# A sliding-window attention and SwiGLU kernel: V's places in SBUF given by the order of their last reading, and x of units 17 to 19 transposed by DMA

## The chip, the core and the metric

The kernel runs on one NeuronCore of one Trainium2 chip, as one launch. The metric is device time in microseconds (us), median of several runs. The engines are named as in the profile: PE is TensorE (PEld its weight loads), DVE is VectorE, ACT is ScalarE, POOL is GpSimd, SP is SyncE. SP and POOL do no arithmetic here: they issue DMAs.

## The reference

Attention with a causal window of 128 and ALiBi slopes over 8 batches, 8 heads, 576 tokens, head size 64, and then a gated MLP over the 4608 tokens:

```python
scores = scale * np.matmul(q, k.transpose(0, 1, 3, 2))
mask = (rel >= 0) & (rel < window)            # rel = query position - key position, window = 128
scores = np.where(mask, scores + bias[None], -1e9)
attn = softmax(scores); attn_out = np.matmul(attn, v)
x = attn_out.transpose(0, 2, 1, 3).reshape(B * S, H * D)     # 4608 x 512
g = x @ w_gate                                # 512 x 1536
val = x @ w_val
out = (silu(g) * val) @ w_out                 # 1536 x 512, float32
```

## The kernel before

The attention is cut into 36 **units** of 128 tokens, `units[i] = (s, p)` with i = 9 s + p: s is a pair of batches, p = 0 to 3 the four whole tiles of the first batch, 4 to 7 those of the second, and p = 8 the two last half tiles of 64 tokens together. A **rank** is the same numbering for loaded tiles of q, k and v (all eight heads, 128 x 512).

A load (`load_qk`, L184, and `load_v`, L179) is a DMA issued by POOL, float32 in HBM to fp16 in SBUF. Tiles of q and k go to the pool `nat`, five places for each. Tiles of v go to twelve fixed places `va_all`, in turn: `va[rank] = va_all[rank % NV]` (L180). POOL issues its DMAs in a fixed order, for each rank k, q, v; it is an in-order queue, so a load whose place isn't free yet holds all loads behind it. No more than eight of POOL's DMAs are in flight, since each waits for the landing of the eighth before it.

From rank 11 on (`QK_DMA_FROM`), q and k are transposed by a DMA that SP issues (L236), into `kT` (12 places) and `qT` (9 places). SP too is an in-order queue; it also issues the stores of the output (L459).

`scores(i)` multiplies kT and qT into four PSUM tiles of the pool `ps_a` (4 places), ACT takes the exponent, VectorE applies the mask. `weighted(i)` (L337) multiplies with `va` into two PSUM tiles `av`, also of `ps_a`; VectorE divides by the sums (L360, L361) and writes the unit's `x`. `x` has three places (`xpool`, tag "x"), so unit i writes where the x of unit i - 3 lay. V of a rank is read by its own unit and the next one; of the ranks with c = 3 (c = rank % 9) it is also read by the unit p = 8 of the same pair, and the same holds for c = 7, which comes right before.

`x_transposed(i)` (L371) brings x into `xT`, the input of the MLP, in blocks of four units (block 8 holds the four units p = 8). For units below `X_DMA_FROM` = 22, PE transposes it in four matmuls into a PSUM tile `px` of `ps_a` (L385) and ACT copies it out (L389). In the generator `attention` this comes one unit late, by the list `waiting` (L894). From unit 22 on SP issues one DMA that transposes x directly (L379).

The MLP goes over nine blocks of 512 tokens: gate and val products (L413, `pg` and `pv`, PSUM pool `ps_f`, three places), tanh on ACT (L431), `uu` and `hT` on VectorE (L432, L443), and the product with w_out by a scheme with seven products for eight (L548), whose sums VectorE makes (L501 to L504). Blocks 6 to 8 do the gate and val products that way as well (L637).

PE's order is written out by hand: `everything` (L983) interleaves the steps of the MLP with those of the attention. POOL's order is fixed too. ACT, VectorE and SP are ordered by a scheduler, which plans with its own estimates of when things are ready; on the chip each engine then follows that order strictly.

Of the kernel before, what the change touches and what calls it, by code (L numbers as in the profile page):

```python
# [16 lines left out]
P = 128  # L17
WIN = 128
QK_DMA_FROM = 11
X_DMA_FROM = 22  # L20
MASKS_AT = (3.0, 5.0, 6.0, 7.0)
ALONE = 8
MANUAL = "compute"
# [27 lines left out]
def kernel(  # L51
# [98 lines left out]
    NV = 12  # L150
    VROW = 80
    va_all = []
# [12 lines left out]
    natq, natk, va = {}, {}, {}  # L165
# [4 lines left out]
    def source(src, rank):  # L170

        s, c = divmod(rank, 9)
        if c == 8:
            return [((64 * n, 64 * n + 64),
                     src[2 * s + n, :, 512:576, :].rearrange("h p d -> p h d")) for n in range(2)]
        b, t = 2 * s + c // 4, c % 4
        return [((0, P), src[b, :, t * P:(t + 1) * P, :].rearrange("h p d -> p h d"))]

    def load_v(rank):  # L179
        va[rank] = va_all[rank % NV]  # L180
        for (p0, p1), src in source(v, rank):
            nc.gpsimd.dma_start(va[rank][p0:p1, :, 0:D], src)  # L182

# [7 lines left out]
    def load(rank):  # L191
        load_qk(rank)
        load_v(rank)
# [143 lines left out]
    def weighted(i):  # L337

        s, p = units[i]
        x = xpool.tile([P, H, D], FP16, name="x", tag="x")  # L340
        xs[i] = x
        for half in range(2):
            pool, tag = (ps_f, "gv") if i < FIRST else (ps_a, "a")
            av = pool.tile([P, 4, D + 1], FP32, name="av", tag=tag)
            todo = []
            for j in range(4):
                h = 4 * half + j
                if p == 8:
                    for n, kt in enumerate((3, 7, 8)):
                        todo.append((j, ex[(s, "c", n)][:, slot(h), :], va[9 * s + kt][:, h, 0:D + 1]))  # L350
                else:
                    if p not in (0, 4):
                        todo.append((j, ex[(s, p - 1)][:, slot(h), 128:256],
                                     va[9 * s + p - 1][:, h, 0:D + 1]))
                    todo.append((j, ex[(s, p)][:, slot(h), 0:128], va[9 * s + p][:, h, 0:D + 1]))
            for n, (j, w, val) in enumerate(todo):
                nc.tensor.matmul(av[:, j, :], w, val, start=(n == 0), stop=(n == len(todo) - 1))  # L357
            rec = xpool.tile([P, 4, 1], FP32, name="rec", tag="rec", bufs=4)
            with tc.high_priority() if i in (6, 7) else ExitStack():
                nc.vector.reciprocal(rec, av[:, :, D:D + 1])  # L360
                nc.vector.tensor_mul(x[:, 4 * half:4 * half + 4, :], av[:, :, 0:D],  # L361
                                     rec.broadcast_to([P, 4, D]))
# [3 lines left out]
    def place(i):  # L366

        s, p = units[i]
        return (8, s) if p == 8 else (2 * s + p // 4, p % 4)

    def x_transposed(i):  # L371
        n, j = place(i)
        if n not in xT:
            xT[n] = bpool.tile([P, NKB, 512], FP16, name="xT", tag="xTc" if n == 8 else "xT",
                               bufs=1 if n == 8 else 3)
        x = xs.pop(i).rearrange("p h d -> p (h d)")
        dst = xT[n][:, :, j * P:(j + 1) * P]
        if i >= X_DMA_FROM:
            nc.sync.dma_start_transpose(dst, x)  # L379
            return  # L380
        pool, tag, n = ((ps_f, "gv", 3) if i == 2 else (ps_f, "po", 1) if i < FIRST
                        else (ps_a, "a", 4))
        pt = pool.tile([P, NKB, P], FP16, name="px", tag=tag, bufs=n)
        for kb in range(NKB):
            nc.tensor.transpose(pt[:, kb, :], x[:, kb * P:(kb + 1) * P], idm if i < FIRST else idm2)  # L385
        if i < FIRST:
            nc.vector.tensor_copy(dst, pt)
        else:
            nc.scalar.copy(dst, pt)  # L389
# [418 lines left out]
    def loads_to(r):  # L808
        nonlocal loaded
        while loaded <= min(r, NR - 1):  # L810
            load(loaded)
            loaded += 1

    def transposes_to(n):
        nonlocal done_t
        while done_t < n:
            transpose(done_t)
            done_t += 1

    def ahead(i):  # L820

        n = need[min(i + 4, last)]
        while done_t < n and order[done_t][1] < loaded and order[done_t][1] >= QK_DMA_FROM:
            transposes_to(done_t + 1)

    def run(steps):
        for fs in steps:
            for f in fs:
                f()
            yield  # L830
# [7 lines left out]
    def first_tiles():  # L838
# [14 lines left out]
        for i in range(FIRST):  # L853
            if i + 1 < FIRST:
                for n, _ in enumerate(run(scores(i + 1))):
                    if n == 0 and i == 0:
                        begin_scores(2, 0, 0)
                        begin_scores(2, 0, 1)
                    if n == 0 and i + 2 < FIRST:
                        transposes_to(need[i + 2])  # L860
            else:
                later_masks()
                for m in range(2):
                    wide(0, m, "g", P)
            weighted(i)
            if 0 < i < FIRST - 1:
                x_transposed(i - 1)
        x_transposed(2)
        begin(4, 2)
        x_transposed(3)  # L870
        begin(4, 3)

    def attention():

        waiting = []
        transposes_to(need[FIRST])
        for _ in run(scores(FIRST)):
            yield FIRST
        for i in range(FIRST, last + 1):
            late = i >= LATE  # L880
            if i < last:
                transposes_to(need[i + 1])
                for n, _ in enumerate(run(scores(i + 1))):
                    yield i - len(waiting)
                    if n == 2 and late:
                        weighted(i)
                        yield i - len(waiting)
            if not late or i == last:
                weighted(i)
                yield i  # L890
            loads_to(i + 7)
            ahead(i)
            yield i - len(waiting)
            if late and i < X_DMA_FROM:  # L894
                if waiting:
                    x_transposed(waiting.pop(0))
                waiting.append(i)
                yield i
                yield i
                continue  # L900
            while waiting:
                x_transposed(waiting.pop(0))
            x_transposed(i)
            yield i
            yield i + 1
# [11 lines left out]
    load_qk(1, "qk")  # L917
    load_qk(2, "q")
    load_v(0)
    load_qk(2, "k")  # L920
    load_qk(3, "q")
    load_v(1)
    load_qk(3, "k")
    load_v(2)
# [32 lines left out]


    att = attention()
    done = n_att = 0  # L960
    ready = [4, 8, 13, 17, 22, 26, 31, 35, 36]
# [88 lines left out]
```

The softmax here doesn't subtract the row's maximum and nothing guards it: scores larger than these inputs give would overflow.

## Time and profile before

| | us |
|---|---|
| median of 3 runs | 336.18 (335.59 to 336.44) |
| profiled execution, its own time | 335.64 |
| span of the profiled execution | 333.9 |
| PE busy | 325.9 |
| VectorE busy | 274.2 |
| ACT busy | 206.9 |
| POOL busy | 111.0 |

The profiled execution's own time is 1.7 us above its span, which runs from the first instruction to the last. Times in the views are counted from the start of the span. A DMA's duration on SP's row is that of its issue; "landing" is when all its data has arrived. A wait is listed as engine, line, releaser, then total, times and longest.

### The profile page before, as it was taken

The page shows a single profiled execution, that of the slowest core. Times are in us where ns is not written, and L with a number is a line of the kernel's source. Part 1 is how long each engine was busy: PE and PEld are TensorE (multiplying, and loading weights), DVE is VectorE, ACT ScalarE, POOL GpSimd, SP SyncE. Part 2 cuts the span into 40 slices and gives each one's busy share as a digit, 9 for nine tenths or more (in the row PEclk, how much of TensorE's full clock was granted, in tenths as well). Part 3 has the DMA queues.
Part 4 walks back from the last instruction along what each step waited for, and adds up shares of the span by engine and source line. Part 5 has one row for each costly group of instructions (what it writes and reads, how often), then busy time and mean ns, then how long its engine had stood idle before and what let it go on. Part 6 is the DMA issues. An engine that isn't in the chain of part 4 may idle for free.

```text
span 333.9 us, 7719 instructions
## 1 busy us (share of the span) xinstructions
PE 325.9 (98%) x2955; PEld 218.5 (65%) x2955; DVE 274.2 (82%) x643; ACT 206.9 (62%) x413; POOL 111.0 (33%) x138
## 2 busy tenths in 40 slices
PE   8999999999999999999999999999999999999994
PEld 4665465544465655656655655666788888888883
DVE  4678878999797879988999999999855985775683
ACT  4976777464766657567456465563567667776650
POOL 8977776458964098551035000000000000000000
PEclk9999999999999999999999999999999999999999
DMA  9999999999999999999969532030100101011014
GB/s 154 175 179 175 177 185 164 122 142 184 141 170 159 140 195 162 160 168 155 179 128 152 117 34 81 16 96 17 65 29 36 64 2 65 25 41 65 0 65 127
DMA packets 161669, 37.64 MB, mean 113 GB/s; under 512 B 149472, under 2 KB 157280, under 8 KB 161632
## 3 DMA queue, kind: packets, MB, share of 16 engines
q0 software_dynamic: 118880, 18.62, 78.8%
q1 hardware_dynamic: 42064, 17.90, 27.8%
q10 hardware_dynamic: 688, 0.62, 0.6%
q8 instruction: 23, 0.38, 0.5%
q14 instruction: 14, 0.11, 0.1%
HBM read 37.91 MB, written 9.44 MB: 142 GB/s over the span
## 4 chain that ended last, share of the span: by engine, by line
PE 87%; DVE 8%; ACT 2%; issue 1%; DVEq 0%
PE po L548 19%; PE pg L413 17%; PE pv L413 16%; PE gX L637 9%; PE av L357 5%; PE gY L637 5%; PE ps L289 3%; PE p L548 3%; PE gZ L637 2%; DVE uu L432 2%; PE psc L325 2%; DVE hT L443 2%; PE po L467 2%; PE px L385 2%; DVE ex L301 1%
## 5 line engine op out<-in xcount | busy, mean ns | idle before, releaser
L413 PE MATMUL pv<-xT,wv_sb 128*128 128x512 f16 (+2 forms) x312 | 76.6, 363 | 0.3 <-DVE uu L432 0.2
L413 PE MATMUL pg<-xT,wg_sb 128*128 128x512 f16 (+2 forms) x324 | 76.5, 355 | 0.1
L431 ACT ACTIVATE tt<-pg 128x512 f16<-128x512 f32 x68 | 40.9, 603 | 44.6 <-PE pg L413 44.6
L295 ACT ACTIVATE ex<-ps 128x512 f16<-128x512 f32 x96 | 50.0, 608 | 7.4 <-PE ps L289 7.4
L432 DVE SCALAR_TENSOR_TENSOR uu<-tt,pg 128x512 f16<-128x512 f16 x67 | 45.6, 681 | 8.6 <-ACT tt L431 8.3
L443 DVE TENSOR_TENSOR hT<-uu,pv 128x512 f16<-128x512 f16 x68 | 46.2, 681 | 1.6
L182 POOL DMA_DIRECT2D va<-in_v_dram x40 | 34.5, 871 | 38.2 <-DMA out_dram<-osb 20.4
L548 PEld LDWEIGHTS <-hT 128*128 128x128 f16 x384 | 37.2, 98 | 10.7 <-issue 0.8
L413 PEld LDWEIGHTS <-wg_sb 128*128 128x128 f16 x324 | 28.5, 98 | 23.5 <-issue 2.2
L413 PEld LDWEIGHTS <-wv_sb 128*128 128x128 f16 x312 | 27.8, 98 | 24.4 <-issue 2.3
L188 POOL DMA_DIRECT2D kn<-in_k_dram x39 | 33.5, 863 | 18.8 <-DMA qT<-qn 6.2
L188 POOL DMA_DIRECT2D qn<-in_q_dram x39 | 33.6, 871 | 9.7 <-DMA va<-in_v_dram 4.7
L548 PEld LDWEIGHTS <-S 128*128 128x128 f16 x288 | 27.5, 98 | 7.5 <-issue 1.4
L301 DVE TENSOR_TENSOR ex<-ex,m_reg 128x1024 f16<-128x1024 f16 x42 | 28.5, 685 | 3.0 <-ACT ex L295 3.0
L361 DVE TENSOR_TENSOR x<-av,rec 128x256 f16<-128x256 f32 x72 | 28.5, 420 | 0.5
L548 PE MATMUL po<-T,S 128*128 128x256 f16 x192 | 25.9, 273 | 0.3 <-ACT u2s L574 0.3
L548 PE MATMUL po<-T,hT 128*128 128x256 f16 x192 | 26.0, 272 | 0.0
L329 ACT ACTIVATE exc<-psc 128x512 f16<-128x512 f32 x40 | 21.4, 608 | 3.2 <-PE psc L325 3.1
L691 DVE TENSOR_TENSOR hT<-s,v 128x512 f16<-128x512 f16 x18 | 7.6, 424 | 17.7 <-ACT s L690 17.7
L357 PEld LDWEIGHTS <-ex 128*128 128x128 f16 x384 | 17.5, 98 | 4.4 <-issue 1.0
L357 PE MATMUL av<-va,ex 128*128 128x65 f16 x384 | 19.3, 193 | 0.3 <-ACT ex L295 0.3
L289 PE MATMUL ps<-qT,kT 64*128 64x256 f16 x192 | 16.0, 272 | 0.9 <-DVE qT L220 0.6
(129 smaller groups left out, 534.1 us busy)
## 6 DMA issues: line engine op xcount, KB each, us to landing
out_dram<-osb SPq DMA_DIRECT2D x32, 256.0 KB, 2.4
va<-in_v_dram POOLq DMA_DIRECT2D x32, 128.0 KB, 6.9
qn<-in_q_dram POOLq DMA_DIRECT2D x31, 128.0 KB, 7.9
kn<-in_k_dram POOLq DMA_DIRECT2D x31, 128.0 KB, 7.3
wg_sb<-in_moe_w_gate_dram POOLq DMA_DIRECT2D x6, 256.0 KB, 7.6
wo_sb<-in_moe_w_out_dram POOLq DMA_DIRECT2D x3, 512.0 KB, 8.2
wv_sb<-in_moe_w_val_dram POOLq DMA_DIRECT2D x5, 256.0 KB, 7.6
kn<-in_k_dram POOLq DMA_DIRECT2D x8, 64.0 KB, 6.4
```

Source lines behind the costliest of these rows:

```text
L182: nc.gpsimd.dma_start(va[rank][p0:p1, :, 0:D], src)
L188: nc.gpsimd.dma_start(t_[p0:p1], src)
L295: nc.scalar.activation(e[:, o:o + 2, :], banks[q4][par], AF.Exp, scale=scale)
L301: nc.vector.tensor_mul(e[:, o, :], e[:, o, :], reg[:, o, :])
L357: nc.tensor.matmul(av[:, j, :], w, val, start=(n == 0), stop=(n == len(todo) - 1))
L361: nc.vector.tensor_mul(x[:, 4 * half:4 * half + 4, :], av[:, :, 0:D], rec.broadcast_to([P, 4, D]))
L413: nc.tensor.matmul(ps[:, c0:c1], w[:, kb, ms], xT[n][:, kb, c0:c1], start=(kb == 0 and c0 == 0), stop=(kb == NKB - 1 and c1 == 512), skip_ ...
L431: nc.scalar.activation(tt, pg[:, c0:c1], AF.Tanh, scale=0.5)
L432: nc.vector.scalar_tensor_tensor(out=uu, in0=tt, scalar=one if (n, m) == PIN else 1.0, in1=pg[:, c0:c1], op0=ALU.add, op1=ALU.mult)
L443: nc.vector.tensor_mul(hT[n][:, m, c0:c1], acted[(n, m)][1][:, c0:c1], pv[:, c0:c1])
L548: nc.tensor.matmul(dst, a[:, m, cols], b[:, m, :], start=(start and m == 0), stop=(m == HM - 1), skip_group_check=True)
L637: nc.tensor.matmul(dst[:, i, :], w[:, kb, c0 + i * P:c0 + (i + 1) * P], a[:, kb, :], start=(start and i == 0 and kb == 0), stop=(i == 1 an ...
```

## The change

`load_v` no longer takes V's places in turn. It keeps for each of the twelve places the unit that reads it last, and gives a new tile the place whose last reading comes first. And `X_DMA_FROM` becomes a set that holds the units 17, 18 and 19 besides 22 to 35, so that these three go by DMA from SP, without `waiting`; units 20 and 21 stay with PE.

```diff
-X_DMA_FROM = 22
+X_BY_DMA = {17, 18, 19} | set(range(22, 36))
...
+    free_at = [-1] * NV
+
     def load_v(rank):
-        va[rank] = va_all[rank % NV]
+
+        n = free_at.index(min(free_at))
+        free_at[n] = rank - rank % 9 + 8 if rank % 9 == 3 else rank + (rank % 9 < 8)
+        va[rank] = va_all[n]
...
-        if i >= X_DMA_FROM:
+        if i in X_BY_DMA:
             nc.sync.dma_start_transpose(dst, x)
             return
...
-            if late and i < X_DMA_FROM:
+            if late and i not in X_BY_DMA:
```

The unit whose reading of V must be over before a rank's V can be loaded, for the ranks where it changes most:

```
rank     15  16  17  18  24  25  26  27  28  30  33  34  35
before    8   5   6   7  17  14  15  16  17  19  26  23  24
after     5   6   7   8  14  15  16  17  17  19  23  24  25
```

What stands in SP's queue, as built (k27 is the transpose of K of rank 27, q27 that of Q, x17 that of unit 17's x, S a store; the start and the end, equal or nearly so, are left out):

```
before  k17 q17 S k18 q18 k19 q19 k20 q20 S k21 q21 k22 q22 k23 S q23 q24 k24 S S k25 q25 k26 q26 S
        k27 q27 k28 S q28 k29 q29 k30 q30 k31 k32 q31 q32 S S x22 q33 x23 k33 x24 S S x25 x26 k34 q34 k35 q35 x27
after   k17 q17 k18 q18 S k19 q19 k20 k21 S q20 S q21 k22 q22 k23 S q23 q24 k24 q25 k25 S k26 q26 S
        k27 q27 x17 k28 q28 k29 k30 x18 S q29 S x19 k31 q30 k32 q31 q32 S S x22 q33 x23 k33 q34 k34 x24 k35 S q35 S x25 x26 x27
```

On PE three groups of four transposing matmuls are gone, on ACT the three copies; the rest of PE's and ACT's order is the same, and VectorE's but for two pairs of neighbours that change places. POOL issues the same DMAs in the same order.

## The prediction

> **What bounds the kernel now.** I read the page's shares first, then the chain that ended last, then the busy times by stage, then the queues of POOL and SP.
>
> ```profile
> PE 325.9 (98%) x2955; PEld 218.5 (65%) x2955; DVE 274.2 (82%) x643; ACT 206.9 (62%) x413; POOL 111.0 (33%) x138
> DMA  9999999999999999999969532030100101011014
> PE 87%; DVE 8%; ACT 2%; issue 1%; DVEq 0%
> ```
>
> TensorE is busy 98% of the span, and the chain lies on it for 87%. The busy times by stage give PE 59.75 of the 60 us from 100 to 160 us: a microsecond for which PE waits is a microsecond of the end, and one that PE saves is saved. The second line says that the DMA engines are full for the first half of the span (20 slices of 8.35 us).
>
> POOL, which issues all loads, waits long twice for a place of V (engine, line, releaser; total, times, longest):
>
> ```profile
> POOL va L182 <- DMA out_dram<-osb: 20.4, 1, 20.4
> POOL va L182 <- PE av L357: 11.7, 2, 9.6
> ```
>
> The 9.6 us end at 116.58 (V of rank 24; its place is rank 12's, which unit 17 reads last, until 115.86), the 20.4 us at 172.27 (rank 33 in rank 21's place, last read by unit 26 until 171.54; the releaser named is not the true one). Nobody on PE waits for either: V of 24 is read at 146.57 and V of 33 at 212.76, 30 and 40 us later. And the DMA engines hardly noticed. In the DMA view of 114 to 120 us, 40 slices of 0.15 us, this is their busy share:
>
> ```profile
> DMA  9111119999999999999999997999999999999999
> ```
>
> Five slices, 0.75 us, are empty. The loads in flight and SP's transposes filled the rest.
>
> SP's queue and VectorE around the change (start, duration; SP's duration is the issue alone):
>
> ```profile
> 132.32 1.24 SPq L236 DMA_TRANSPOSE kT<-kn  x1
> 133.67 1.28 SPq L236 DMA_TRANSPOSE qT<-qn  x1
> ...
> 147.87 1.19 SPq L236 DMA_TRANSPOSE kT<-kn  x1
> 149.17 1.22 SPq L236 DMA_TRANSPOSE qT<-qn  x1
> ```
> ```profile
> 136.92 0.76 DVE L361 TENSOR_TENSOR x<-av,rec 128x256 f16<-128x256 f32 x2
> 137.59 0.41 DVE L504 TENSOR_TENSOR S<-hT,S 128x512 f16<-128x512 f16 x1
> 137.92 0.68 DVE L432 SCALAR_TENSOR_TENSOR uu<-tt,pg 128x512 f16<-128x512 f16 x1
> ...
> 141.32 0.76 DVE L361 TENSOR_TENSOR x<-av,rec 128x256 f16<-128x256 f32 x2
> ```
>
> Counted along the queue, the first two are K and Q of rank 27, the next two K and Q of rank 30. The two writes of x are units 20 and 21. Landing, in the answer for line 236 from 127 to 152 us, and for line 379 over the span:
>
> ```profile
> DMA to landing us min/median/max: 6.3/7.0/8.9
> ```
> ```profile
> DMA to landing us min/median/max: 2.4/2.4/5.6
> ```
>
> A transpose by DMA takes 7.0 us while loads run, and 2.4 us after them. The new ones fall into the first stretch.
>
> **What the Trainium skill says.** "DMA: Bandwidth & Descriptors", section "Issuing engines are not separate DMA queues": DMAs of SP and POOL run on the same 16 engines and interleave. The trace agrees: 7.0 against 2.4 us. "Perfetto Trace Analysis", "DMA Instruction — HWDGE": the profiled window of such an instruction is its issue, not the moving of data. It agrees: 1.19 us against 6.8 us for the transpose at 147.87. "TensorE: Matmul & The Clock Gate", Part 1: after an idle window of about 3.4 us the array runs at half clock until it has been busy as long. At the start of this trace seven matmuls of 512 columns took 3.17 us, 453 ns each, where four in mid-kernel take 0.86 us, 215 ns each.
>
> **The change, part by part.**
>
> *PE and ACT.* Twelve transposing matmuls go. One group of four costs 0.22 us on the chain:
>
> ```profile
> 131.09 0.22 PE px L385 x4
> 131.32 0.86 PE pg L413 x4
> ```
>
> Three groups: 0.67 us off PE. Three copies of 0.585 us leave ACT, 5.6 to 6.9 us busy of ten there: worth nothing to the end. The orders of PE, ACT and VectorE are otherwise the same but for two neighbour swaps on VectorE, worth nothing.
>
> *V's places.* Rank 24 now waits for unit 14 instead of 17, rank 33 for 23 instead of 26; rank 27 waits for 17 instead of 16, 34 and 35 for one unit more. For PE directly: nothing, covered by the 30 and 40 us. For what stands behind in POOL's queue (K and Q of 25 and on): these are paced by the DMA engines. The 0.75 us of empty slices and the two microseconds after, in which the share of the DMA falls to 1.3 from its usual 1.9, make about 1.4 us; K of rank 30 comes earlier by that, less about 0.6 us for x17 (131 KB at some 200 GB/s) ahead of it. Bounds: 0 and 3 us earlier (3.0 is the pause in landings, from Q of 24 at 117.9 to V of 24 at 120.9). I take 0.9: K of rank 30 is issued at 147.0.
>
> *The three transposes on SP.* Each takes 1.3 us of SP and waits for its x. What matters is where they stand: x17 behind K and Q of rank 27, x18 behind K of rank 30, x19 five places later (store, Q of 29, store between). SP issues in order, and those before wait for loads. x17: 132.32 - 0.9 + 1.3 + 1.3 = 134.0 us, though its x is ready at 118.04. x18: 147.0 + 1.3 = 148.3 us, ready at 124.97. Landing 7.2 and 6.4 us later (within 6.3 to 8.9): 141.2 and 154.7 us.
>
> *Who waits for that.* x has three places, so unit 20 writes where x17 lay, 21 where x18, 22 where x19; before, PE had read them by 125.2, 131.3 and 136.4. Now VectorE waits for the landing, and all its queue with it. Unit 20's write, 136.92 before, goes to 141.2. Queued behind it is uu (137.92 before), which frees the PSUM place of the pv at 140.07: PE stands there some 3 us. Unit 21's write, 141.32 before, goes to 154.7. That write also frees unit 21's two av places in PSUM, and the second of the score matmuls of unit 23 takes the first of these. They were here:
>
> ```profile
> 143.64 0.61 PE L289 MATMUL ps<-qT,kT 64*128 64x256 f16 x8
> ```
>
> The second starts near 143.70; now it can at 154.7 + 0.42 (one write) + 0.05 = 155.2. PE is 11.5 us late, and this includes the first stall and the 0.67 us, which only lengthen the wait. The pg after it (144.84) needs hT, queued behind x21 (1.37 us from its start to hT's end): 156.1 against PE's own 156.3, no more. Unit 22's write would stand at 159.6; x19 is issued 3.9 us after x18, at 152.2, and lands by 159.1: just hidden.
>
> *Clock.* PE stands about 3 us and then 8: after the second the skill's page has it at half clock for some 3.4 us, 1.7 us of work. No run here shows it in mid-kernel; bounds 0 and 3.2 (both stalls). I take 1.5.
>
> Sum: 335.64 + 11.5 + 1.5 = 348.6 us for the profiled execution, and the median of the runs lies 0.54 above that execution: **349.1 us**.
>
> **Rivals.**
> 1. *No stall* (the other side): SP gets to the new transposes early, because POOL no longer stands 9.6 us. For it: that wait is right there. Against it: the DMA engines were full meanwhile. It decides at x18 landing by 143.70 - 0.67 - 0.47 = 142.6, that is K of rank 30 issued by 134.9, 13 us earlier than now; 9.6 us isn't enough. Then only the 0.67 us remain, and perhaps 0.24 us of score matmuls that waited for places at 137.2: 335.3 us in the median.
> 2. *Loads gain it all*: K of rank 30 comes 9.6 us earlier, at 138.3; x18 lands at 146.6, PE is 3.4 us late, without a clock loss: 339.6. Against it, the same DMA row.
> 3. *The lag goes on*: x19 lands late too, and VectorE, busy 29.9 of 30 us from 160 to 190, can't make up its lag; another 3 to 6 us: 352 to 355.
> That the change doesn't do what it says is excluded by the built order: twelve matmuls fewer, three more transposes on SP, VectorE's three writes waiting for them.
>
> **How the numbers follow.** The stall as worked out 0.76, rival 3 0.06, rival 2 0.11, rival 1 0.07. A measurement of this kernel can tell about 0.3%, 1.0 us: rival 1 lies just inside, so faster 0.03, same 0.04, slower 0.93. For the likeliest case: early end, K of 30 comes 3 us earlier, a landing of 6.3 us, no clock loss: x18 at 152.5, 9.2 us late, 345.4; late end, no gain, 0.6 us more for x17, a landing of 8.9 us and 3.2 us of clock: 158.7, 15.4 + 3.2, 354.8. The range 343 to 354 holds nearly all of that and part of rivals 2 and 3.
>
> **What would show it.** Right: VectorE idle before x at units 20 and 21, some 4 and 9 us, released by the DMA of xT; PE idle at pv or uu near 140 and at ps near 144, near 11 us in all; a dip in PEclk after it; POOL's two long waits for va gone; x18 issued right behind a kT at about 147. Wrong: kT of rank 30 issued before 140, no idle on VectorE, or a PE that runs through it.

## The result, and the profile after

| | before | after |
|---|---|---|
| median, us | 335.71 (335.28 to 336.44, 6 runs) | 349.16 (348.66 to 349.99, 6 runs) |
| profiled execution, its own time | 335.64 | 349.19 |
| its span | 333.9 | 347.4 |

The ratio is 1.0401, its 95% interval 1.0384 to 1.0419: 13.45 us slower, where 349.1 us had been predicted. In all tables of this document medians and ranges count every execution; the ratios leave out two, 341.83 us of v_alone and 341.86 us of x_5_places, as slow (each lies over 1.5% above the fastest of its kernel). In the changed kernel every line number from L180 on is 5 higher (x is written at L366, its transpose by DMA is issued at L384, the score matmuls are L294). "Late" below always means: later than the same instruction in the kernel before.

From the page of the changed kernel: the busy times; PE and its clock in 40 slices of 8.7 us; the chain that ended last.

```profile
PE 329.9 (95%) x2943; PEld 219.2 (63%) x2943; DVE 274.2 (79%) x643; ACT 205.9 (59%) x410; POOL 111.1 (32%) x138
PE   8999999999999997649999999999999999999994
PEclk9999999999999999688999999999999999999999
PE 69%; DVE 11%; DMA 11%; issue 3%; ACT 3%; POOL 1%; SPq 0%; DVEq 0%; POOLq 0%
```

PE has twelve matmuls fewer and is nevertheless busy 4 us longer, because part of them ran at a lower clock. It has a hole in three slices, between 130 and 156 us. DMA, absent from the chain of before, has 11% of it.

Waits (engine, line, releaser; total, times, longest):

```profile
POOL va L187 <- PE av L362: 23.6, 4, 16.3
DVE x L366 <- DMA xT<-x: 12.0, 2, 7.8
PE ps L294 <- DVE x L366: 9.6, 2, 4.9
```

The two lower lines are the mechanism: VectorE may not write a new x where an old one lies that a transpose by DMA is still reading; it waits twice for such a transpose, and PE then waits for VectorE. (The lower clock comes on top of that.) Next, SP's queue, VectorE and PE in the timeline (start, duration, what, and in brackets the idle time ahead of it and what ended it):

```profile
132.78 1.25 SPq L241 DMA_TRANSPOSE qT<-qn  x1
134.12 1.34 SPq L384 DMA_TRANSPOSE xT<-x  x1
...
141.35 5.24 SPq L241 DMA_TRANSPOSE kT<-kn  x2
146.68 1.99 SPq L384 DMA_TRANSPOSE xT<-x  x1
...
151.42 1.26 SPq L384 DMA_TRANSPOSE xT<-x  x1
```
```profile
141.17 0.76 DVE L366 TENSOR_TENSOR x<-av,rec 128x256 f16<-128x256 f32 x2 [4.17 <-DMA xT<-x]
...
154.47 0.76 DVE L366 TENSOR_TENSOR x<-av,rec 128x256 f16<-128x256 f32 x2 [7.83 <-DMA xT<-x]
```
```profile
136.55 0.39 PE L294 MATMUL ps<-qT,kT 64*128 64x256 f16 x4
141.65 0.94 PE L294 MATMUL ps<-qT,kT 64*128 64x256 f16 x4 [4.70 <-DVE x L366]
142.51 1.89 PE L418 MATMUL pg<-xT,wg_sb 128*128 128x512 f16 x4
...
149.82 0.28 PE L294 MATMUL ps<-qT,kT 64*128 64x256 f16 x1
...
154.95 1.03 PE L294 MATMUL ps<-qT,kT 64*128 64x256 f16 x7 [4.86 <-DVE x L366]
155.91 1.46 PE L553 MATMUL po<-wo_sb,S 128*128 128x256 f16 x6
157.17 1.91 PE L418 MATMUL pg<-xT,wg_sb 128*128 128x512 f16 x4
...
161.08 1.03 PE L418 MATMUL pg<-xT,wg_sb 128*128 128x512 f16 x4
```

x17 is issued behind Q of rank 27, x18 behind K of rank 30 (the second of the two K that share a row), x19 behind a store. They land near 141.1, 154.4 and 158.6. The writes of units 20 and 21 follow the first two within 0.1 us. PE stops in the middle of the score matmuls of unit 22, and again after the first of unit 23's; after each stop four matmuls of 512 columns take 1.9 us and not 1.03. Unit 23's second score matmul starts at 154.95, before at 143.64, in a pair with the first: 11.31 us late. VectorE's hT that stood at 150.01 before is 13.61 us late, and so is each later one up to the last, which stood at 228.31: nothing is made up, and nothing more is lost.

### The profile page after: what moved, and what is told of

Its sections match the earlier page's. It is cut to its first block, busy times and chain, and to the rows that moved or that the text cites. A ratio compares the mean times of both kernels' runs of the same rounds, so it can differ in the third digit from the quotient of the medians.

```text
span 347.4 us, 7707 instructions
## 1 busy us (share of the span) xinstructions
PE 329.9 (95%) x2943; PEld 219.2 (63%) x2943; DVE 274.2 (79%) x643; ACT 205.9 (59%) x410; POOL 111.1 (32%) x138
## 4 chain that ended last, share of the span: by engine, by line
PE 69%; DVE 11%; DMA 11%; issue 3%; ACT 3%; POOL 1%; SPq 0%; DVEq 0%; POOLq 0%
PE po L553 15%; PE pg L418 12%; PE pv L418 11%; PE gX L642 9%; PE gY L642 5%; DMA kn<-in_k_dram 4%; PE av L362 3%; DMA va<-in_v_dram 3%; DVE uu L437 3%; PE ps L294 3%; PE p L553 2%; DVE hT L448 2%; PE gZ L642 2%; DMA xT<-x 2%; DMA qT<-qn 2%
## 5 line engine op out<-in xcount | busy, mean ns | idle before, releaser
L418 PE MATMUL pg<-xT,wg_sb 128*128 128x512 f16 (+2 forms) x324 | 78.2, 362 | 0.1
L187 POOL DMA_DIRECT2D va<-in_v_dram x40 | 34.2, 861 | 31.3 <-PE av L362 23.6
L366 DVE TENSOR_TENSOR x<-av,rec 128x256 f16<-128x256 f32 x72 | 28.4, 419 | 12.5 <-DMA xT<-x 12.0
L294 PE MATMUL ps<-qT,kT 64*128 64x256 f16 x192 | 17.1, 279 | 10.4 <-DVE x L366 9.6
L553 PE MATMUL po<-T,S 128*128 128x256 f16 x192 | 26.6, 277 | 0.3 <-ACT u2s L579 0.3
L294 PEld LDWEIGHTS <-kT 64*128 64x128 f16 x192 | 8.0, 95 | 21.8 <-DVE x L366 10.7
```

Source lines behind the costliest of these rows:

```text
L294: nc.tensor.matmul(two[par][:, j, :], kT[rows, ks, pair, :], qT[rows, p:p + 2, pair, :], start=(j == 0 and not early_tile), stop=(j == 1))
L418: nc.tensor.matmul(ps[:, c0:c1], w[:, kb, ms], xT[n][:, kb, c0:c1], start=(kb == 0 and c0 == 0), stop=(kb == NKB - 1 and c1 == 512), skip_ ...
L553: nc.tensor.matmul(dst, a[:, m, cols], b[:, m, :], start=(start and m == 0), stop=(m == HM - 1), skip_group_check=True)
```

## The experiments

Three theories stood at the start. **A**: x by DMA lands late, and the three places of x make VectorE, then PE, stand. **B**: V's places themselves cost the time. **C**: a transpose by DMA costs something wherever it stands. Kernels measured together share their runs of the kernel before; the column "before" has the median of these.

**Each part alone.**

```diff
v_alone:  +X_BY_DMA = set(range(22, 36))        # V's places by last reading, x as before
x_alone:  -        va[rank] = va_all[n]
          +        va[rank] = va_all[rank % NV]  # V in turn, x of 17 to 19 by DMA
```

> V's places by the order of their last reading, x of units 17 to 19 again by PE. Theory A (x by DMA lands late, and x's three places make VectorE and then PE stand): same as before, 335.7 us, since nobody on PE waited for V; POOL's waits of 9.6 and 20.4 us shorter. Rival B (V's places themselves cost the 13 us, by rank 27 and its followers waiting longer): near 349. Rival C (every transpose by DMA costs, wherever it stands): same as before.

> x of units 17 to 19 by DMA, V's places in turn as before. In the built order x17 now stands ahead of K of rank 25, x18 behind Q of 26, x19 behind K of 29: earlier in SP's queue than with both parts together. Theory A: x17 is issued near 122 and lands near 128, x18 near 131.5 and 138, both ahead of their need (136.5 and 140.9): no stall. x19 is issued near 146 and lands near 152.5, against a need at 147.4: PE stands some 3 us at the score matmuls of unit 24. 338.5 us, between 336 and 340. Rival B: same as before, 335. Rival C: near 349.

| | median, us | before | ratio, 95% |
|---|---|---|---|
| v_alone | 337.12 (334.94 to 341.83, 20 runs) | 335.75 | 1.0019 to 1.0059 |
| x_alone | 341.23 (337.92 to 342.54, 6 runs) | 335.75 | 1.0118 to 1.0192 |

Alone the parts cost 1.4 and 5.5 us, together 13.45. They act on each other by way of SP's queue. With V in turn the scheduler places the three transposes like this, against the order with both parts:

```
x_alone     S S x17 k25 q25 k26 q26 x18 S k27 q27 k28 S q28 k29 x19 q29 k30
both parts      k25 S k26 q26 S k27 q27 x17 k28 q28 k29 k30 x18 S q29 S x19 k31
```

In x_alone x17 and x18 are out early, and only x19, issued at 145.99, lands late for unit 22's write. That was expected, though not the size: the time lies above the range of A. The transpose lands at 153.31 instead of 152.5, PE stands 3.69 us instead of 3, and the clock falls after the stop here too.

```profile
153.41 0.42 DVE L366 TENSOR_TENSOR x<-av,rec 128x256 f16<-128x256 f32 x1 [5.49 <-DMA xT<-x]
```

v_alone wasn't expected to cost anything. Its executions fall in two groups, ten below 336.6 and ten above 337.6 us, so the median between them tells little; the profiled one (339.45) belongs to the upper group and shows one wait, of unit 25's write for the transpose of unit 22:

```profile
171.01 0.76 DVE L366 TENSOR_TENSOR x<-av,rec 128x256 f16<-128x256 f32 x2 [4.35 <-DMA xT<-x]
```

That transpose was issued at 161.91 and took 9.01 us to land; before, issued at 161.34, it took 3.20. The busy times by stage say why. One row each, of before and of v_alone; behind the five engines stand PEclk, the load of the DMA engines as it is counted there (it can exceed 1), and GB/s:

```profile
162.00:171.00 9.00, 9.00 (x86) 4.95 (x84) 9.00 (x23) 5.76 (x13) 0.00 (x0) 1.00 0.71 171
```
```profile
162.00:171.00 9.00, 6.55 (x66) 3.70 (x64) 4.66 (x12) 4.84 (x10) 2.84 (x5) 1.00 1.67 176
```

Before, POOL stood from about 152 to 172.27 us for a place of V, no load was on the way after 160.9, and unit 22's transpose had the DMA engines nearly to itself. Take that wait away and the loads lie on top of the transpose: DMA 1.67 for 0.71. PE then stands too, and the clock falls:

```profile
171.50 0.94 PE L294 MATMUL ps<-qT,kT 64*128 64x256 f16 x4 [2.94 <-DVE x L366]
172.42 1.87 PE L418 MATMUL pg<-xT,wg_sb 128*128 128x512 f16 x4
```

**Places of x.** The same kernel with four and with five places of x. They need room, which the op pool gives up (6 for 7).

```diff
+    opool = ctx.enter_context(tc.tile_pool(name="op", bufs=6))
+        x = xpool.tile([P, H, D], FP16, name="x", tag="x", bufs=5)   # x_4_places: bufs=4
```

> The changed kernel with four places for x instead of three (and six instead of seven for the output tiles, to make room). The orders of all engines' instructions stay. Theory A: unit 21 now waits for x17 (landed 141.2 against a need at 140.9: nothing), unit 22 for x18 (landed 154.4 against 147.4): PE stands at the score matmuls of unit 24 until 154.9 instead of 149.6, and loses some clock: 342 us, between 339 and 344. Rivals B and C: 349.

> The changed kernel with five places for x (and six for the output tiles). Theory A: unit 22 waits for x17, unit 23 for x18 (154.4 against a need near 153.8), unit 24 for x19 (158.5 against 160): next to nothing. 335.2 us, between 334.6 and 336.3, and PE 0.67 us less at work than before. Rivals B and C: 349. If it lies near 335 the six places of the output tiles cost nothing either.

| | median, us | before | ratio, 95% |
|---|---|---|---|
| x_4_places | 342.76 (341.59 to 344.69, 6 runs) | 335.75 | 1.0186 to 1.0245 |
| x_5_places | 336.03 (335.29 to 341.86, 22 runs) | 335.75 | 0.9999 to 1.0021 |

With four places unit 21 writes where x17 lay, and unit 22 where x18 lay; only the latter waits:

```profile
154.32 0.43 DVE L366 TENSOR_TENSOR x<-av,rec 128x256 f16<-128x256 f32 x1 [5.93 <-DMA xT<-x]
```

With five places, and the transposes as late on SP as before (x17 at 132.87, x18 at 147.34, x19 at 151.29), VectorE waits for none, and 13.2 of the 13.45 us are gone. That settles A against B and C: late transposes as such cost no more than a few tenths of a microsecond (ratio 0.9999 to 1.0021); what costs is the write of x that waits for them.

**One transpose at a time.**

```diff
only_17:  +X_BY_DMA = {17} | set(range(22, 36))
only_18:  +X_BY_DMA = {18} | set(range(22, 36))
```

> The changed kernel with x of unit 17 alone by DMA (18 and 19 by PE). Theory A: x17 lands near 141.2, PE stands as in the changed kernel from 136.7 to 141.6, some 4.2 us beyond before's own pace there, and loses about 1.4 us by the clock after it: 341.3 us, between 340 and 343. If the loss were a third of the whole for each of the three transposes: 340.

> The changed kernel with x of unit 18 alone by DMA. Theory A: x18 still stands behind K of rank 30, is issued near 145.4 and lands near 153; PE stands once, from about 143 to 153.5, and then loses 1.9 us by the clock: 347.4 us, between 345 and 349: nearly the whole loss, since x17's stall only lies ahead of x18's. If the loss were a third of the whole for each: 340.

| | median, us | before | ratio, 95% |
|---|---|---|---|
| only_17 | 342.90 (342.21 to 343.63, 4 runs) | 335.45 | 1.0198 to 1.0245 |
| only_18 | 348.67 (348.23 to 350.07, 4 runs) | 335.45 | 1.0375 to 1.0426 |

VectorE's waits in the two traces, only_17 first:

```profile
142.25 0.76 DVE L366 TENSOR_TENSOR x<-av,rec 128x256 f16<-128x256 f32 x2 [5.23 <-DMA xT<-x]
```
```profile
153.60 0.76 DVE L366 TENSOR_TENSOR x<-av,rec 128x256 f16<-128x256 f32 x2 [12.03 <-DMA xT<-x]
```

x17 alone costs 7.5 us and x18 alone 13.2, but both with x19 13.45: they don't add up. Unit 21's write goes when x18 lands, near 154 us, whether unit 20's has waited before or not; of its 12 us the first stall takes 4.

**The clock.** Idle matmuls keep PE busy ahead of the score matmuls of units 22 and 23; first 20 and 28, then 20 and 18, since the 28 ended at 158.1, two microseconds after x18 had landed (156.0). (From the score matmuls on, line numbers are 3 higher again.)

```diff
+                for _ in range({22: 20, 23: 18}.get(i, 0) if q4 == 0 else 0):   # fill_pe: 23: 28
+                    nc.tensor.matmul(two[0].rearrange("p a q -> p (a q)"), idm2, idle,
+                                     start=True, stop=True)
```

> The changed kernel with matmuls of no use ahead of the score matmuls that wait: 20 of 512 columns at unit 22, 28 at unit 23, into the first score tile, which the real matmuls then overwrite. PE is busy in most of the stall. Clock as a cause of its own: no dip of the granted clock, and the 1.9 us after the second stall go: 347.3 us, between 346.8 and 347.8. Rival: PE is slow after the stall because VectorE and ACT must catch up: 349.2, or more.

> As fill_pe, but with 18 idle matmuls in place of 28 ahead of unit 23's score matmuls, so that they end before x18 lands (fill_pe's ended 1.5 us after). The idle matmuls write places that the score matmuls then overwrite. Read by the lateness against the kernel before: in the changed kernel unit 21's write of x is 13.15 us late and the last hT of block 5 13.55 (start of the execution taken out). Theory P, of the prediction: PE's lateness at unit 23's second score matmul sets the end, about 1.9 us less than that of unit 21's write, and all of the half clock counts: the last hT some 1.9 us less late than unit 21's write, the time 347.2 (346.7 to 347.7) for the same landing. Theory V: VectorE, which has almost no idle time there, carries its own lateness on, and the half clock costs only what it adds to that: the last hT 0.4 us less late than unit 21's write, the time 348.3 (347.9 to 348.7).

> The changed kernel once more, as the measure for fill_18 in the same call: 349.2 us (348.8 to 349.6) by both theories, the last hT 0.3 to 0.5 us later than unit 21's write.

| | median, us | before | ratio, 95% |
|---|---|---|---|
| fill_pe | 348.10 (346.23 to 350.00, 4 runs) | 335.45 | 1.0324 to 1.0391 |
| fill_18 | 348.90 (347.01 to 349.34, 4 runs) | 335.43 | 1.0346 to 1.0423 |
| after_again | 348.48 (348.10 to 348.87, 4 runs) | 335.43 | 1.0355 to 1.0419 |

The medians decide nothing. fill_pe lies above the range that a kept clock was to give; in its traced execution PE still stood 3.28 us at unit 22 when the 20 were through, and the clock fell there. The landing of x18 differs by as much between executions (153.0 us in after_again, 154.4 in the first trace, 156.0 in fill_pe) as the clock is worth, and in three of fill_18's four executions the mean clock was below full again. Only its profiled execution (347.01) kept the clock, and there the lateness can be read. The row of the page, and PE around the second stall:

```profile
PEclk9999999999999999999999999999999999999999
```
```profile
154.42 0.72 PE L297 MATMUL ps<-qT,kT 64*128 64x256 f16 x7 [2.38 <-DVE x L369]
155.67 0.82 PE L556 MATMUL po<-wo_sb,S 128*128 128x256 f16 x6 [0.53 <-DVE osb L561]
156.33 1.03 PE L421 MATMUL pg<-xT,wg_sb 128*128 128x512 f16 x4
```

| late by, us (start of the execution taken out) | unit 21's write of x | the hT at 150.01 before | difference |
|---|---|---|---|
| after | 13.09 | 13.55 | +0.46 |
| after_again | 11.86 | 12.73 | +0.87 |
| only_18 | 12.06 | 13.22 | +1.16 |
| fill_18, clock kept | 12.21 | 11.07 | -1.14 |

The half clock is thus worth 1.6 to 2.3 us of the end (-1.14 against +0.46 to +1.16). The other three executions of fill_18, whose clock was not kept, took 1.9 to 2.3 us longer, but where their transposes landed is not known. after_again's difference lies above the 0.3 to 0.5 expected of it, so the range is wide. Neither theory of this pair came out exact: with the clock kept PE was 10.37 us late at the second score matmul, and not all of the end follows from that, as theory P had it, nor does VectorE carry on its 12.21 less 0.4, as V had it. The second line above shows the middle: po waits 0.53 us for a sum that stands in VectorE's delayed queue. It is one execution, so the size is rough. Nor has the half clock one price: where a single write waited, the same difference is about +1.5 us in only_17 and x_4_places, +0.9 in x_alone and nothing in v_alone, though the clock fell in all four. What these would be at full clock no run shows.

**Is there anything to be gained?** V in turn with x by DMA; V by last reading without x by DMA; and the kernel before: each with five places of x and the op pool of six.

```diff
in_turn_5:   x_5_places with va[rank] = va_all[rank % NV]
v_5_places:  x_5_places with X_BY_DMA = set(range(22, 36))
before_5:    before with x bufs=5, op bufs=6
```

> V's places in turn as in the kernel before, x of units 17 to 19 by DMA, and five places of x (op pool 6 for 7, to make room). With V in turn the scheduler puts x17 to x19 further forward in SP's queue, and the write of x that each place waits for comes two units later. Theory A: no wait of VectorE for xT is left, and the 12 px groups saved show: 0.67 us less than before, 334.8 us (334.3 to 335.5). Theory C, that each transpose by DMA costs something wherever it stands: 336.0 or more, as with both parts and five places (336.03).

> V's places by last reading, x by DMA from unit 22 on only, five places of x (op pool 6). Theory A: what V's places cost alone (337.12 for 335.75, with executions near 336 and others near 338.5) is unit 25's write of x waiting for unit 22's transpose; with five places that wait is gone, and every execution lies at the time of before: 335.5 us (335.0 to 336.0). Theory B, that V's order costs by itself (POOL's loads, K and Q): still 337 us, with executions above 338.

> The kernel before with five places of x and six of the op pool for seven, nothing else. No write of x waits for a transpose in the kernel before, so all theories expect its time: 335.5 us (335.2 to 335.9). Above that, the smaller op pool costs what is seen here, and the 0.67 us that both parts with five places should have gained is lost to it.

| | median, us | before | ratio, 95% |
|---|---|---|---|
| in_turn_5 | 335.45 (335.07 to 336.14, 22 runs) | 336.00 | 0.9963 to 0.9992 |
| v_5_places | 335.18 (334.83 to 335.99, 22 runs) | 336.00 | 0.9954 to 0.9982 |
| before_5 | 335.62 (334.97 to 336.27, 22 runs) | 336.00 | 0.9964 to 0.9994 |

v_5_places has no execution above 336.0, though unit 22's transpose took 7.4 us beside the loads in its trace: with no write of x waiting, V's places cost nothing, and theory B falls for good. The three lie within 0.44 us of one another, so neither part of the change, freed of its wait, gives more than about 0.1%. All three are 0.2 to 0.3% below the kernel before, by about as much as a measurement can tell. In this measurement a part of the executions of before lay near 337 us, while none of the 66 of the others was above 336.3; that before sometimes waits for unit 22's transpose too, and five places take that away, is argued only, since no execution of before near 337 us was traced.

in_turn_5 was expected to show the twelve saved matmuls, 0.67 us. It doesn't. PE and VectorE of in_turn_5 near 137 us:

```profile
136.29 0.39 PE L294 MATMUL ps<-qT,kT 64*128 64x256 f16 x4
137.19 0.72 PE L294 MATMUL ps<-qT,kT 64*128 64x256 f16 x4 [0.51 <-DVE x L366]
```
```profile
136.49 0.25 DVE L365 RECIPROCAL rec<-av 128x4 f32<-128x4 f32 x2
136.71 0.76 DVE L366 TENSOR_TENSOR x<-av,rec 128x256 f16<-128x256 f32 x2
```

PE comes early to unit 22's score matmuls and waits 0.51 us for unit 20's write, which VectorE, without a gap since before 131 us, makes no sooner than ever. In before_5 the same eight matmuls run from 136.77 without a wait that the view lists (in 0.96 us, where unit 23's eight took 0.61). Each hT of in_turn_5 from 143.7 us on is 0.17 us later than in before_5, to the last one, and so is the first at 21 us: of the 0.67 us nothing is left. Theory C doesn't explain it either, as the time, 335.45, is below its 336.0.

## Why the prediction was right, and where its steps were off

*SP and the landings: right.* x17 was put at 134.0 with landing at 141.2 (134.12 and 141.1), x18 at 148.3 and 154.7 (146.68 and 154.4), x19 at 152.2 and by 159.1 (151.42 and 158.6). For x18 two errors cancelled: the issue came 1.6 us sooner, since K of rank 30 gained 2.5 us and not 0.9, and the landing took 7.7 us and not 6.4, the duration of the transposes ahead of it in before. That they cancelled is luck. The step that mattered, that loads freed by V's places would not bring SP there 10 us sooner, held: 2.5 us lies inside the bounds of 0 and 3. These bounds were somewhat too tight, though: in the other nine traces with V's new places K of rank 30 was issued between 144.0 and 147.8 us, 0.1 to 3.8 us before the 147.87 of the kernel before. (The five slices of the DMA row that the prediction calls empty stand at 1, about a tenth busy; that changes its 1.4 us little.)

*Unit 21's write and PE's second score matmul of unit 23: right.* 11.5 us late were predicted, counted from a start near 143.70, and 11.31 measured, and only_18 shows that this wait alone makes nearly all of it. *x19 just hidden: right*, by 2.6 us (unit 22 writes at 161.18) where 0.5 were predicted.

*The first stall: wrong in place and size, without effect on the sum.* The prediction followed unit 20's write to uu and put 3 us at the pv of 140.07. PE stood 4.70 us, and earlier, at unit 22's score matmuls: they take the av place that unit 20's write frees. That is the same rule which the prediction used one unit later, for unit 23. only_17 gives this stall's own price, 7.5 us. It vanishes beneath the second, as the prediction said. The second stop took 4.86 us and not 8, since PE came to it late from the first; the lateness behind it is nearly the predicted one.

*The clock: right in kind, 1.5 us against 1.6 to 2.3.* The Trainium skill, "TensorE: Matmul & The Clock Gate", Part 1, has the array fall to half clock after an idle window of about 3.4 us. These traces agree in the main: idle times of 4.70 and 4.86 us halved the clock, 0.51 us did not. But 2.94 us did as well (v_alone; its next four gate matmuls took 1.87 us), and 2.38 us in fill_18 did not; the measurement decides, and in these traces the limit lies between these two. In the changed kernel PE then worked at half clock for 4.5 and 4.8 us (141.65 to 146.1 and 154.95 to 159.8), not 3.4, so that the term was somewhat too small.

*The 0.67 us saved on PE: wrong.* The step "a microsecond for which PE waits is a microsecond of the end, and one that PE saves is saved" fails in its second half. VectorE is nearly as tight there, and its write of unit 20 takes the gain back within two microseconds of the third group (in_turn_5). In the changed kernel the term had no part in the sum.

*"V's places: for PE directly nothing": right for PE, incomplete for the DMAs.* v_5_places shows that the places cost nothing in themselves. Missed were that POOL's 20.4 us of standing had kept the DMA engines free for unit 22's transpose (v_alone, 1.4 us), and that V's places move x17 to x19 back in SP's queue, which makes 5.5 us into 13.45. The built order that the prediction used had the latter in it, so its numbers did.

*"POOL's two long waits for va gone": wrong in the changed kernel*, which has 23.6 us in four waits, the longest 16.3. PE, standing, gives V's places back later. Where PE doesn't stand, in x_5_places, it is 8.0 us in three, the longest 4.8:

```profile
POOL va L187 <- PE av L362: 8.0, 3, 4.8
```

*Rivals.* No stall (335.3) and loads that gain all (339.6) are out by x18's issue at 146.68; the lag that goes on (352 to 355) by the constant 13.6 us from 150 us on.

## What to carry to other kernels

Moving a transpose from a compute engine to a DMA queue changes when its *source* comes free: count the places of the source, find the write that will take this place, and hold it against issue plus landing under the load of that moment (about 7 us here), not against the time at which the result is needed. Places enough for the landing (five for three) took away the whole cost, while the transposes stayed as late as they were. And a long wait on a queue that nobody waits for may still be of use to others: POOL's 20 us of standing was what let unit 22's transpose land in 3.2 us for 9.0.

## What the runs showed that was not expected

The two parts, 1.4 and 5.5 us alone, cost 13.45 us together, because with V's new places the scheduler puts x17 to x19 further back in SP's queue. A transpose of x by DMA took 2.4 us to land on nearly idle DMA engines and up to 9.0 us beside loads, the issue being about 1.2 us in both. The half clock set in after 2.94 us of idle PE. And twelve matmuls fewer on the engine that is busy for 98% gained nothing: what in_turn_5 saved on it came back as a wait for an engine that the page shows at 82%.
